# A gate handed out in two parts, six relayout transfers, single copies of R and V, and other windows for the background work

## The chip, the cores and the metric

The kernel runs on one core of a Trainium2 chip. The metric is the time of one execution on the device in microseconds (us). A core has engines that each work through their own instruction stream in order: TensorE (PE; its weight loads are listed as PEld), VectorE (DVE), ScalarE (ACT), GpSimd (POOL) and SyncE (SP), which here issues most transfers. Semaphores tie the streams together.

## The reference

Two stages in fp32. The first is a recurrence over 768 time steps for 4 batches of 8 heads, with a 40x40 state for each; the second an MLP over the 3072 tokens.

```python
for t in range(S):
    y[:, :, t] = np.einsum('bhd,bhde->bhe', rt, state)
    Sa = np.einsum('bhde,bhe->bhd', state, at)
    state_decay = state * wt[:, :, None, :] - np.einsum('bhd,bhe->bhde', Sa, bt)
    state = state_decay + np.einsum('bhd,bhe->bhde', vt, kt)
...
h = x @ w_in                       # 3072x320 by 320x2048
g = np.where(pos, h, np.where(neg, 0.0, (h + beta) ** 2 / (4.0 * beta)))
return (g @ w_out)                 # 2048 by 320
```

## The kernel before

The time steps are cut into 24 **chunks** of 32; four chunks are a **set** (0 to 5). Each chunk is worked in two halves of 16 heads.

The **chain** (`chain`) carries the state through a chunk's half in five steps of small matmuls with evictions on VectorE and ScalarE between them (L515, L525, L541, L552, L581). It needs, for the chunk, rows of a scratch in DRAM (`scr`): `load_ti` (L312, tiles `ti`) and `load_cg` (L441, L444, tiles `cg`), issued on SP; `turn` transposes them on VectorE.

The **background** prepares each set in three kinds of work, which run while earlier chunks are in the chain:
- *rows* (`prelude`): four parts a set. A part scales the inputs: a copy on ScalarE (L268), two scans on VectorE (L244), the copy of P on ScalarE (L278), three products on POOL (L279, L288, L295) and a 640 KB store to `scr` from POOL (L296). In each part `copy_rv` (L142, SP) copies a piece of R and one of V from the inputs to `scr`, 160 KB each.
- *ab* (`ab_set`): for each of four chunks a load of `tiab` by four transfers (L312), and two halves, each with two transposes on VectorE (L325), 32 small matmuls (L334) and a copy on ScalarE (L340).
- *inverse* (`invert`): after a transpose (L350) 31 steps of a product and a difference on POOL (L361, L367); `adopt` (L375) hands the result over when the set begins.

The **MoE** (`moe`) takes 64 time steps as a group (12 groups), in 8 pairs of 128-row blocks of the hidden layer. `relayout` brings a finished group's y into `X` by transfers on SP. For a pair: the first products (16 matmuls, L630, into `ph`), the gate (relu L638 and square L639 on ScalarE, minimum and maximum L640 on VectorE), its split into a high part (`gh`, L646, ScalarE) and a low part (`gl`, L647, POOL), and the second products (12 matmuls, L659). The second products of a pair are issued after the first products of the pair that follows: first products of pair k, gate of k, second products of k-1, split of k, first products of k+1.

The **order** is fixed in the program. The main loop goes through each chunk in four stages; after each it calls `fill`, which has six steps. In each step `feed(1280)` takes MoE instructions worth 1280 columns (a fill is one pair), then weights are converted by `wgen` (in the first chunks), and `background` issues rows, ab and inverse work. How much is told by `WINDOWS`: a position counts 10 for a chunk, and a kind of work of a set is spread evenly between the two positions of its window, by the weights that its generator yields (`ROWS_W`, `AB_W`, `INV_W`). The weights `AB_W[5]` and `AB_W[4]` stand after a load of `tiab` and set how much of the window passes before its first use.

Of the kernel before, what the change touches and what calls it, by code (L numbers as in the profile page):

```python
# [20 lines left out]
NB, NHD, D, L = 4, 8, 40, 32  # L21
NH = NB * NHD
# [6 lines left out]
    rows=[(0, 0), (24, 43), (38, 58), (66, 98), (106, 138)],  # L29
    ab=[(0, 0), (46, 55), (63, 79), (103, 119), (143, 159)],  # L30
    inv=[(5, 36), (55.5, 79), (81, 118), (121, 158), (161, 198)],
# [9 lines left out]
AB_W = (1, 16, 1, 4, 28, 20)  # L41
# [13 lines left out]
def rwkv_moe_kernel(ctx: ExitStack, tc: tile.TileContext, r, k, v, w, a, b, w_in, w_out, ident_d, mask_d, out):  # L55
# [83 lines left out]
    def copy_rv(s, part, c):  # L139

        x, o = ((r, O_R), (v, O_V))[part]
        nc.sync.dma_start(  # L142
            scr4[s][c, :, :, o : o + D], x.rearrange("b h (n t) e -> (b h) n t e", t=L)[:, 4 * s + c]
        )
# [103 lines left out]
    def prelude(s):  # L248
# [17 lines left out]
        for part in range(4):  # L266
# [16 lines left out]
            for i in range(2):  # L283
                copy_rv(s, i, part)
# [307 lines left out]
    def relayout(g):  # L592
# [7 lines left out]
        for i, (f, p) in enumerate(((0, 0), (1, 0), (0, 2))):  # L600
            nc.sync.dma_start(
                Xb[40 * i : 40 * i + 40, 0:4, :].rearrange("e c (b t) -> e (c b) t", b=NB),
                yf[64 * f : 64 * f + D, p : p + 2].rearrange("e p j b t -> e (p j b) t"),
            )
        for i in range(2):
            for q in range(2):
                nc.sync.dma_start(  # L607
                    Xb[40 * i : 40 * i + 40, 4 + q, :].rearrange("e (b t) -> e b t", b=NB), yf[64 : 64 + D, 2 + i, 0]
                )
        for q in range(2):  # L610
            nc.sync.dma_start(
                Xb[80:120, 4 + q, :].rearrange("e (b t) -> e b t", b=NB), yf[64 : 64 + D, 2 + q, 1]
            )
        return X
# [6 lines left out]
    def moe():  # L621
# [13 lines left out]
        def gate(k):  # L635
# [3 lines left out]
            nc.scalar.activation(gt, gt, AF.Square)  # L639
            nc.vector.scalar_tensor_tensor(out=gt, in0=gt, scalar=1.0, in1=ph, op0=ALU.min, op1=ALU.max)  # L640
            return gt
# [26 lines left out]
        for g in range(len(groups)):  # L668
            while g not in Xs:
                yield None  # L670
            for k in range(NF // 2):
# [5 lines left out]
                new = (g, k, gate(k))  # L677
                if late:
                    yield from second(*late)
                else:  # L680
                    yield 3840
# [131 lines left out]
    for c in range(1, 4):  # L813
        at(1, lambda c=c: [early_store(0, c)] + [copy_rv(0, i, c) for i in range(2)])
# [31 lines left out]
    steps += [[lambda i=i: copy_rv(1, i % 2, i // 2)] for i in range(8)] + [[lambda: pad_scr(1)]]  # L846
# [115 lines left out]
```

## Time and profile before

| | us |
|---|---|
| median of 3 runs | 881.17 |
| lowest and highest | 880.77, 887.12 |
| profiled execution, its own time | 879.51 |
| its span, first to last instruction | 877.6 |
| busy: PE, PEld | 701.3, 642.4 |
| busy: DVE, ACT, POOL | 591.9, 419.6, 441.0 |
| transfers, all queues | 122.01 MB in 222363 packets |

Busy time is the sum of an engine's instructions; since engines work side by side, the shares don't add up. A line of the page such as "L647 POOL TENSOR_TENSOR gl<-gt,gh" names the line of the kernel, the engine, the operation and the tiles. "Idle before" an instruction is time in which its engine stood still, and the name behind the arrow is what ended it. The granted clock is TensorE's, as a share of full speed (1.00 is 2.4 GHz, 0.50 is 1.2 GHz).

### The profile page before, as it was taken

The numbers are of one execution on the slowest core, as the hardware profiler recorded it, in microseconds if no ns is written. First come the engines' busy times: TensorE is split into PE (matmuls) and PEld (weight loads), VectorE is DVE, ScalarE is ACT, GpSimd is POOL, SyncE is SP. The second block draws the span as 40 slices with busy tenths as digits, with TensorE's granted clock in tenths as the row PEclk, the third lists the DMA queues.
The fourth block names the chain that finished last, engine by engine and source line by source line (L and its number), as shares of the span: only waits on it lengthen the run. The fifth ranks groups of instructions, "written<-read, shape, count | busy, mean of one in ns | idle before, by whom it ended". The sixth has DMA issues, their size and how long they took to land.

```text
span 877.6 us, 35507 instructions
## 1 busy us (share of the span) xinstructions
PE 701.3 (80%) x15360; PEld 642.4 (73%) x15360; DVE 591.9 (67%) x1338; ACT 419.6 (48%) x888; POOL 441.0 (50%) x621
## 2 busy tenths in 40 slices
PE   4225566686575996999887999888999999999994
PEld 4224555675564886888776888777899899999994
DVE  6895789778663875797475796675876777676210
ACT  6206455555531553455353455443455555555552
POOL 0300289976522587656674457763247752222331
PEclk9665656678776998999898999998999999999998
DMA  8996599888778579658577668666453554551000
GB/s 288 193 216 173 117 199 209 200 201 197 166 160 159 113 156 162 142 142 185 108 154 146 148 162 173 125 127 124 87 123 69 117 107 100 102 117 31 33 18 16
DMA packets 222363, 122.01 MB, mean 139 GB/s; under 512 B 143048, under 2 KB 214920, under 8 KB 222208
## 3 DMA queue, kind: packets, MB, share of 16 engines
q1 hardware_dynamic: 215936, 98.12, 54.4%
q0 software_dynamic: 6272, 21.63, 8.9%
q8 instruction: 121, 1.98, 1.0%
q14 instruction: 34, 0.28, 0.1%
HBM read 90.54 MB, written 27.53 MB: 135 GB/s over the span
## 4 chain that ended last, share of the span: by engine, by line
PE 48%; DVE 15%; DMA 9%; POOL 9%; SPq 7%; issue 6%; ACT 6%; DVEq 0%; ACTq 0%; POOLq 0%
PE ph L630 15%; PE po L659 14%; PE p L552 5%; DMA tiab<-scr 4%; PE p L541 3%; PE p L515 2%; POOL gl L647 2%; PE p L581 2%; SPq L312 2%; POOL lw L361 2%; PE p L525 2%; PE p L481 2%; POOL lw L367 2%; PE p L202 2%; SPq L607 2%
## 5 line engine op out<-in xcount | busy, mean ns | idle before, releaser
L647 POOL TENSOR_TENSOR gl<-gt,gh 128x512 fp32r<-128x512 f32 x96 | 125.1, 1304 | 226.3 <-ACT gh L646 226.3
L630 PE MATMUL ph<-X,w 120*128 120x256 f32 x1536 | 222.8, 298 | 4.7 <-issue 2.7
L630 PEld LDWEIGHTS ph<-X,w 120*128 120x128 f32 x1536 | 200.1, 199 | 12.8 <-issue 3.1
L659 PE MATMUL po<-w,gh 128*128 128x320 f32 x768 | 140.2, 327 | 15.9 <-ACT gh L646 15.9
L640 DVE SCALAR_TENSOR_TENSOR gt<-gt,ph 128x512 f32<-128x512 f32 x96 | 65.8, 685 | 108.9 <-ACT gt L639 91.7
L659 PEld LDWEIGHTS po<-w,gh 128*128 128x128 f32 x768 | 122.0, 200 | 19.0 <-ACT gh L646 18.3
L536 ACT ACTIVATE cg<-p 32x160 f32<-32x160 f32 x192 | 56.6, 295 | 103.3 <-PE p L525 60.2
L638 ACT ACTIVATE gt<-ph,half_c 128x512 f32<-128x512 f32 x96 | 66.0, 687 | 68.2 <-PE ph L630 67.7
L659 PE MATMUL po<-w,gl 128*128 128x320 f32 x384 | 81.4, 337 | 18.8 <-POOL gl L647 18.7
L559 DVE SCALAR_TENSOR_TENSOR cg<-p,pr 40x160 f32<-40x160 f32 x184 | 58.8, 320 | 50.8 <-PE p L552 48.8
L367 POOL TENSOR_TENSOR lw<-lw 128x31 f32<-128x31 f32 (+15 forms) x155 | 87.0, 561 | 8.5
L361 POOL TENSOR_TENSOR lw<-lw 128x31 f32<-128x31 f32 (+15 forms) x155 | 82.8, 534 | 9.3
L493 DVE TENSOR_TENSOR cg<-p,mask 32x256 f32<-32x256 f32 x192 | 80.6, 420 | 3.7 <-PE p L481 0.3
L659 PEld LDWEIGHTS po<-w,gl 128*128 128x128 f32 x384 | 65.3, 206 | 23.9 <-POOL gl L647 23.6
L552 PE MATMUL p<-cg 128*64 128x72 f32 (+1 forms) x1536 | 66.1, 246 | 0.0
L546 ACT COPY ss<-p 40x320 f32<-40x320 f32 x92 | 38.6, 420 | 55.1 <-PE p L541 53.6
L646 ACT CAST gh<-gt 128x512 fp32r<-128x512 f32 x96 | 59.6, 621 | 10.5 <-DVE gt L640 9.5
L639 ACT ACTIVATE gt<-gt 128x512 f32<-128x512 f32 x96 | 60.6, 632 | 3.1
L552 PEld LDWEIGHTS p<-cg 128*64 128x64 f32 x1536 | 60.5, 154 | 0.4 <-issue 0.4
L532 DVE SCALAR_TENSOR_TENSOR cg<-p,mask 32x128 f32<-32x128 f32 x192 | 55.2, 288 | 6.6 <-ACT cg L536 0.9
L581 PEld LDWEIGHTS p<-pr,ss 40*40 40x40 f32 x1472 | 35.7, 129 | 27.5 <-issue 20.8
L325 DVE STREAM_TRANSPOSE ea<-tiab 128x256 f32<-128x256 f32 x64 | 24.3, 418 | 46.3 <-DMA tiab<-scr 45.1
(94 smaller groups left out, 1077.7 us busy)
## 6 DMA issues: line engine op xcount, KB each, us to landing
ti<-scr SPq DMA_DIRECT2D x96, 200.0 KB
ti<-scr SPq DMA_DIRECT2D x96, 168.0 KB
scr<-arena POOLq DMA_DIRECT2D x16, 640.0 KB, 6.0
cg<-scr SPq DMA_DIRECT2D x96, 80.0 KB
X<-Y SPq DMA_DIRECT2D x36, 160.0 KB
scr<-wide SPq DMA_DIRECT2D x8, 640.0 KB
w<-in_moe_w_out_dram POOLq DMA_DIRECT2D x16, 320.0 KB, 5.4
tiab<-scr SPq DMA_DIRECT2D x32, 160.0 KB
```

The costliest lines, as they stand in the source:

```text
L361: eng.tensor_mul(t3, W3[:, 0:n, j : j + 1].broadcast_to([128, n, m]), L3[:, j + 1 :, j].unsqueeze(1).broadcast_to([128, n, m]),)
L367: eng.tensor_sub(W3[:, 0:n, j + 1 :], W3[:, 0:n, j + 1 :], t3)
L493: nc.vector.tensor_tensor(out=cg[q, f::2, C_X : C_X + 64][:, 4 * i : 4 * i + 4].rearrange("p h (j x) -> p h j x", x=32), in0=ps[quarter(f, ...
L552: nc.tensor.matmul(psv[h // 8][64 * f : 64 * f + 64, h // 2 % 4, 0:n3], lhsT=cgw[:, h * CW + C_G : h * CW + C_G + 64], rhs=cg[:, h, C_R : ...
L559: nc.vector.scalar_tensor_tensor(out=cn[er[f], f::2, C_S : C_S + D][:, halves[i]], in0=psv[i][er[f], :, 32:72], scalar=-1.0, in1=pr[er[f], ...
L630: nc.tensor.matmul(phs[k % 2][:, n * j : n * j + n], lhsT=wt[0, f // 4, wi // 2][:, wi % 2, fs], rhs=Xs[g][:, xi, :], start=i == 0, stop=i ...
L638: nc.scalar.activation(gt, ph, AF.Relu, bias=half_c, scale=0.5)
L639: nc.scalar.activation(gt, gt, AF.Square)
L640: nc.vector.scalar_tensor_tensor(out=gt, in0=gt, scalar=1.0, in1=ph, op0=ALU.min, op1=ALU.max)
L646: nc.scalar.copy(gh, gt)
L647: nc.gpsimd.tensor_sub(gl, gt, gh.bitcast(F32))
L659: nc.tensor.matmul(pos[i], lhsT=x[:, ts_], rhs=w, start=q == 0 and k == 0, stop=end)
```

## The change

Five edits. The gate is a generator in two parts: relu and square are issued after the fourth, minimum and maximum after the ninth of the second products of the pair ahead (before, all three stood ahead of the first of them). `relayout` makes six transfers of a group and not nine, with the same bytes. `copy_rv` copies R of a whole set in the first rows part and V in the second, 640 KB each; for set 0 three chunks of R, then three of V, after the three stores of rows; for set 1 one copy of each. The windows of rows, ab and inverse are others. `AB_W[4]` and `AB_W[5]` are 46 and 40 and not 28 and 20.

```diff
--- before.py
+++ after.py
@@ -26,9 +26,9 @@
 
 
 WINDOWS = dict(
-    rows=[(0, 0), (24, 43), (38, 58), (66, 98), (106, 138)],
-    ab=[(0, 0), (46, 55), (63, 79), (103, 119), (143, 159)],
-    inv=[(5, 36), (55.5, 79), (81, 118), (121, 158), (161, 198)],
+    rows=[(0, 0), (24, 43), (46, 64), (70, 90), (106, 130)],
+    ab=[(0, 0), (46, 55), (68, 84), (95, 119), (135, 159)],
+    inv=[(5, 36), (55.5, 79), (85, 118), (121, 158), (161, 198)],
 )
 
 AHEAD = 5
@@ -38,7 +38,7 @@
 SLOTS = len(SHARE)
 
 ROWS_W = (2, 2, 4, 2, 6, 6, 8)
-AB_W = (1, 16, 1, 4, 28, 20)
+AB_W = (1, 16, 1, 4, 46, 40)
 INV_W = 12
 
 TRAIL = 2.5
@@ -136,11 +136,12 @@
                 ident[rows].unsqueeze(1).broadcast_to([D, 8, D]),
             )
 
-    def copy_rv(s, part, c):
+    def copy_rv(s, part, c, n=1):
 
         x, o = ((r, O_R), (v, O_V))[part]
         nc.sync.dma_start(
-            scr4[s][c, :, :, o : o + D], x.rearrange("b h (n t) e -> (b h) n t e", t=L)[:, 4 * s + c]
+            scr[s][0 : NH * 128].rearrange("(h x) e -> h x e", x=128)[:, L * c : L * (c + n), o : o + D],
+            x.rearrange("b h t e -> (b h) t e")[:, 128 * s + L * c : 128 * s + L * (c + n), :],
         )
 
     def pad_scr(s):
@@ -280,8 +281,8 @@
             yield 1
             scan(wz, wz, dz, -1)
             rec = rows_(wz)[:, 2:10]
-            for i in range(2):
-                copy_rv(s, i, part)
+            if part < 2:
+                copy_rv(s, part, 0, 4)
             yield ROWS_W[2]
             bl = load("b", part)
             yield ROWS_W[3]
@@ -602,15 +603,12 @@
                 Xb[40 * i : 40 * i + 40, 0:4, :].rearrange("e c (b t) -> e (c b) t", b=NB),
                 yf[64 * f : 64 * f + D, p : p + 2].rearrange("e p j b t -> e (p j b) t"),
             )
+        lo = Xb[:, 4:6, :].rearrange("e q (b t) -> e q b t", b=NB)
         for i in range(2):
-            for q in range(2):
-                nc.sync.dma_start(
-                    Xb[40 * i : 40 * i + 40, 4 + q, :].rearrange("e (b t) -> e b t", b=NB), yf[64 : 64 + D, 2 + i, 0]
-                )
-        for q in range(2):
             nc.sync.dma_start(
-                Xb[80:120, 4 + q, :].rearrange("e (b t) -> e b t", b=NB), yf[64 : 64 + D, 2 + q, 1]
-            )
+                lo[40 * i : 40 * i + 40], yf[64 : 64 + D, 2 + i, 0].unsqueeze(1).broadcast_to([D, 2, NB, nt])
+            )
+        nc.sync.dma_start(lo[80:120], yf[64 : 64 + D, 2:4, 1])
         return X
 
     MM1 = ((0, 0), (1, 0), (0, 1), (2, 2), (3, 2), (2, 3), (4, 4), (5, 5))
@@ -637,8 +635,9 @@
             gt = mp.tile([128, 512], F32, tag="gt", name="gt", bufs=2)
             nc.scalar.activation(gt, ph, AF.Relu, bias=half_c, scale=0.5)
             nc.scalar.activation(gt, gt, AF.Square)
+            yield gt
             nc.vector.scalar_tensor_tensor(out=gt, in0=gt, scalar=1.0, in1=ph, op0=ALU.min, op1=ALU.max)
-            return gt
+            yield
 
         def split(gt):
             gh = mp.tile([128, 512], F32R, tag="gh", name="gh", bufs=1)
@@ -674,11 +673,13 @@
                 if late:
                     late += split(late[2])
                 yield from first(g, k)
-                new = (g, k, gate(k))
-                if late:
-                    yield from second(*late)
-                else:
-                    yield 3840
+                parts = gate(k)
+                for i, d in enumerate(second(*late) if late else (320,) * 12):
+                    yield d
+                    if i == 3:
+                        new = (g, k, next(parts))
+                    elif i == 8:
+                        next(parts)
                 late = new
         yield from second(*late, *split(late[2]))
 
@@ -811,7 +812,9 @@
     todo = {}
     at = lambda n, f: todo.setdefault(n, []).append(f)
     for c in range(1, 4):
-        at(1, lambda c=c: [early_store(0, c)] + [copy_rv(0, i, c) for i in range(2)])
+        at(1, lambda c=c: early_store(0, c))
+    for i in range(2):
+        at(1, lambda i=i: copy_rv(0, i, 1, 3))
     for k in range(AHEAD):
         at(2, lambda k=k: raw_load(k))
     at(10, lambda: [turn(0, 0, j) for j in (1, 2, 0)])
@@ -843,7 +846,7 @@
     steps += [[lambda part=part: turn_1(1, part)] for part in range(4)]
     steps += [[lambda half=half: early_ab(1, half)] for half in range(2)] + [[lambda: init_cg(2, 2)]]
     steps += [[lambda c=c: early_store(1, c)] for c in range(4)]
-    steps += [[lambda i=i: copy_rv(1, i % 2, i // 2)] for i in range(8)] + [[lambda: pad_scr(1)]]
+    steps += [[lambda i=i: copy_rv(1, i, 0, 4)] for i in range(2)] + [[lambda: pad_scr(1)]]
     first = [lambda x=x: [f() for f in x] for x in steps]
 
     def feed(cols):
```

Line numbers of the changed kernel are one higher up to the gate and a few lower or higher behind it. The first place is VectorE in the first fill of chunk 7 (L463 and L465 of the kernel before turn `ti`; L244 are scans of a rows part, L325 transposes of an ab half, L640 the gate's minimum and maximum, L583 belongs to the chain). Before:

```order
L463 STREAM_TRANSPOSE ev<-ti_83 128x512
L465 STREAM_TRANSPOSE pr_88<-ti_83 128x16x32
L325 STREAM_TRANSPOSE ea<-tiab 128x256 x2
L244 SCALAR_TENSOR_TENSOR wz<-wz,dz 128x400
L640 SCALAR_TENSOR_TENSOR gt<-gt,ph_64 128x512
L325 STREAM_TRANSPOSE ea<-tiab 128x256 x2
L583 SCALAR_TENSOR_TENSOR cg_85<-p_4692,pr_89 40x8x32 x2
```

And now:

```order
L464 STREAM_TRANSPOSE ev<-ti_83 128x512
L466 STREAM_TRANSPOSE pr_88<-ti_83 128x16x32
L326 STREAM_TRANSPOSE ea<-tiab 128x256 x4
L273 MEMSET dz 128x40
L245 SCALAR_TENSOR_TENSOR ld_w<-wz,dz 128x400
L277 COPY dz<-ld_w 128x40
L278 RECIPROCAL dz<-ld_w 128x40
L245 SCALAR_TENSOR_TENSOR wz<-wz,dz 128x400
L639 SCALAR_TENSOR_TENSOR gt<-gt,ph_64 128x512
L584 SCALAR_TENSOR_TENSOR cg_85<-p_4609,pr_89 40x8x32 x2
```

The rows part's scans and four transposes stand ahead of the gate's instruction, where two transposes and the second scan stood; the first scan of that part was in the chunk before.

The second place is ScalarE in the first two fills of chunk 9 (L519, L536 and L571 belong to the chain, L646 is the cast to the high part, L638 and L639 the gate's relu and square). Before:

```order
L519 COPY x_5735<-p_5734 128x288
L646 CAST gh<-gt 128x512
L268 COPY wz<-ld_w 128x8x40
L638 ACTIVATE gt<-ph_64,half_c 128x512
L639 ACTIVATE gt<-gt 128x512
L278 COPY arena<-ld_w 128x8x40
L571 CAST Y<-yt 128x2x4x32
L536 ACTIVATE cg_85<-p_5835 32x4x40 x2
L536 ACTIVATE cg_85<-p_5834 32x4x40 x2
```

And now:

```order
L520 COPY x_5704<-p_5703 128x288
L645 CAST gh<-gt 128x512
L636 ACTIVATE gt<-ph_64,half_c 128x512
L637 ACTIVATE gt<-gt 128x512
L572 CAST Y<-yt 128x2x4x32
L537 ACTIVATE cg_85<-p_5793 32x4x40 x2
L537 ACTIVATE cg_85<-p_5792 32x4x40 x2
```

The two copies of a rows part, L268 and L278, are gone from this chunk.

The third place is SP in chunk 7 (`scr_109` is the scratch of set 4, `scr_108` that of set 3; L664 stores the output). Before:

```order
L664 DMA out_dram<-ob 2x64x320 x2
L142 DMA scr_109<-in_r_dram 32x32x40
L142 DMA scr_109<-in_v_dram 32x32x40
L260 DMA ld_b<-in_b_dram 128x1x320
L312 DMA tiab<-scr_108 32x16x80
L312 DMA tiab<-scr_108 32x16x48
L312 DMA tiab<-scr_108 32x16x80
L312 DMA tiab<-scr_108 32x16x48
L260 DMA ld_w<-in_w_dram 128x1x320
L260 DMA ld_a<-in_a_dram 128x1x320
```

And now, with the single copy of R:

```order
L663 DMA out_dram<-ob 2x64x320 x2
L261 DMA ld_w<-in_w_dram 128x1x320
L261 DMA ld_a<-in_a_dram 128x1x320
L261 DMA ld_k<-in_k_dram 128x1x320
L148 DMA scr_109<-in_r_dram 10x4
L142 DMA scr_109<-in_r_dram 4096x1x40
L313 DMA tiab<-scr_108 32x16x80
L313 DMA tiab<-scr_108 32x16x48
L313 DMA tiab<-scr_108 32x16x80
L313 DMA tiab<-scr_108 32x16x48
L261 DMA ld_b<-in_b_dram 128x1x320
L261 DMA ld_w<-in_w_dram 128x1x320
```

The second load of `tiab` stands straight behind the copy of R, where copies of R and V and a load of b stood.

## Rows read from the trace of the kernel before

**Rows 1.** The page's busy time of each engine, with its share of the span and its instructions.

```profile
PE 701.3 (80%) x15360; PEld 642.4 (73%) x15360; DVE 591.9 (67%) x1338; ACT 419.6 (48%) x888; POOL 441.0 (50%) x621
```

**Rows 2.** Busy time of each engine by stretch, one for each chunk (from ScalarE's first copy L519 of the chunk to that of the next): chunks 7 to 15 one by one, then 18 and 19. The columns are the stretch, its length, the busy time and instructions of PE, PEld, DVE, ACT and POOL, the granted clock, the DMA share and GB/s.

```profile
334.30:373.75 39.45, 31.61 (x719) 28.47 (x718) 25.10 (x61) 15.38 (x36) 26.22 (x39) 0.87 0.74 149
373.75:399.60 25.85, 24.92 (x561) 22.98 (x562) 23.89 (x51) 15.02 (x33) 15.12 (x20) 1.00 0.64 155
399.60:434.05 34.45, 28.59 (x561) 26.27 (x562) 20.34 (x49) 14.39 (x30) 23.11 (x36) 0.85 0.66 142
434.05:464.70 30.65, 28.17 (x657) 25.66 (x658) 21.53 (x55) 16.02 (x35) 20.73 (x28) 0.94 0.73 146
464.70:503.05 38.35, 30.73 (x721) 27.79 (x722) 24.55 (x59) 15.49 (x36) 17.73 (x25) 0.91 0.75 152
503.05:528.90 25.85, 24.91 (x561) 22.97 (x562) 23.88 (x51) 15.00 (x33) 15.63 (x23) 1.00 0.68 159
528.90:561.30 32.40, 27.73 (x561) 25.48 (x561) 20.48 (x48) 14.38 (x30) 23.24 (x33) 0.89 0.68 146
561.30:589.60 28.30, 26.69 (x657) 24.20 (x658) 19.81 (x51) 14.55 (x33) 19.69 (x27) 1.00 0.74 139
589.60:625.00 35.40, 30.55 (x721) 27.73 (x722) 21.35 (x55) 14.11 (x33) 11.52 (x19) 0.90 0.49 97
...
676.10:702.10 26.00, 24.85 (x561) 22.99 (x562) 17.87 (x45) 13.76 (x31) 19.64 (x27) 1.00 0.52 110
702.10:726.50 24.40, 24.40 (x561) 22.89 (x562) 17.82 (x45) 12.97 (x29) 11.58 (x19) 1.00 0.49 97
```

**Rows 3.** Who waited for whom in the whole span: engine, line and what it waited for, then us in total, how often, the longest.

```profile
DVE gt L640 <- ACT gt L639: 91.7, 40, 4.2
ACT gt L638 <- PE ph L630: 67.7, 73, 2.7
...
DVE ea L325 <- DMA tiab<-scr: 45.1, 11, 9.0
...
PE p L334 <- DVE ea L325: 32.8, 14, 12.0
...
PE po L659 <- POOL gl L647: 18.7, 11, 6.1
...
PE po L659 <- ACT gh L646: 15.9, 12, 4.0
```

**Rows 4.** Chunk 9: five instructions of the timeline (start, length, engine, line, in brackets the idle time before it and what ended it), and two stretches as in rows 2.

```profile
399.44 2.18 PE L630 MATMUL ph<-X,w 120*128 120x256 f32 x16
...
403.10 0.69 DVE L640 SCALAR_TENSOR_TENSOR gt<-gt,ph 128x512 f32<-128x512 f32 x1 [1.64 <-ACT gt L639]
...
406.18 0.81 ACT L278 COPY arena<-ld_w 128x320 f32<-128x320 f32 x1 [3.17 <-DVE wz L244]
...
409.25 2.17 PE L659 MATMUL po<-w,gh 128*128 128x320 f32 x8 [1.70 <-ACT gh L646]
...
428.52 1.43 PE L659 MATMUL po<-w,gl 128*128 128x320 f32 x4 [4.16 <-POOL gl L647]
...
424.30:428.50 4.20, 0.06 (x1) 0.00 (x0) 0.99 (x2) 0.27 (x1) 3.96 (x7) 0.79 0.50 154
428.50:431.00 2.50, 2.48 (x38) 2.15 (x38) 0.00 (x0) 0.00 (x0) 1.90 (x3) 0.50 0.00 0
```

**Rows 5.** Chunk 7, timeline: SP's issues of copies, of b and of `tiab`, and the transpose on VectorE that waits for the last.

```profile
332.77 1.21 SPq L142 DMA_DIRECT2D scr<-in_r_dram  x1
334.02 3.68 SPq L142 DMA_DIRECT2D scr<-in_v_dram  x1
337.80 2.75 SPq L260 DMA_DIRECT2D ld_b<-in_b_dram  x1
340.65 2.13 SPq L312 DMA_DIRECT2D tiab<-scr  x4
...
347.72 0.77 DVE L325 STREAM_TRANSPOSE ea<-tiab 128x256 f32<-128x256 f32 x2 [6.95 <-DMA tiab<-scr]
```

**Rows 6.** Set 2's ab, timeline: SP's copy and load, and the first of PE's products that waited.

```profile
237.03 0.64 SPq L142 DMA_DIRECT2D scr<-in_r_dram  x1
...
238.57 1.76 SPq L312 DMA_DIRECT2D tiab<-scr  x3
...
244.95 0.68 PE L334 MATMUL p<-ea 40*32 40x32 f32 x32 [12.05 <-DVE ea L325]
```

**Rows 7.** Groups of instructions by line and form: the matmuls of all 32 halves of ab; busy us, mean ns, idle before.

```profile
L334 PE MATMUL p<-ea 40*32 40x32 f32 x1024 | 18.0, 206 | 44.4 <-DVE ea L325 32.8 <-DVE cg L583 11.6
```

**Rows 8.** A quiet fill late in the chain, timeline: the end of the gate and the cast that follows it.

```profile
810.11 0.69 DVE L640 SCALAR_TENSOR_TENSOR gt<-gt,ph 128x512 f32<-128x512 f32 x1 [0.94 <-POOL gl L647]
...
812.45 0.62 ACT L646 CAST gh<-gt 128x512 fp32r<-128x512 f32 x1
```

**Rows 9.** The issues of L607 (duration least, median, most; first and last start) and, in the tail's timeline, the two waits of PE for the last group's relayout.

```profile
L607 SPq DMA_DIRECT2D X<-Y x48: 706/707/1442, 148.3 to 831.3; - x48
...
834.10 0.38 PE L630 MATMUL ph<-X,w 120*128 120x256 f32 x1 [0.28 <-DMA X<-Y]
...
834.85 1.33 PE L630 MATMUL ph<-X,w 120*128 120x256 f32 x9 [0.36 <-DMA X<-Y]
```

**Rows 10.** The page's list of DMA issues: the store of a rows part, KB and median us from issue to landing.

```profile
scr<-arena POOLq DMA_DIRECT2D x16, 640.0 KB, 6.0
```

## The prediction

> **What bounds the kernel now.** I read the page's head first: TensorE is busy 80% of the span [rows 1], so it is a race between one long instruction stream and what holds it up. The second view is the table of stretches, cut by chunk of 32 time steps [rows 2]. In it the reader should see a floor: chunk 19, in which only the chain and the MoE run, takes 24.40 us with PE busy throughout and a granted clock of 1.00. Chunks with background work stand above it, and unevenly: chunk 8 at 25.85, chunk 9 at 34.45, chunk 11 at 38.35, chunk 15 at 35.40. The number of PE's main instructions hardly differs, so the excess is waiting and what follows from it. Third, the table of waits [rows 3]: PE stood 32.8 us before L334's products for DVE's transposes of `tiab`, and DVE itself 45.1 us for the load of `tiab`; PE stood 18.7 and 15.9 us before the second products for the low and the high part of the gate. Last, the timeline of one bad chunk [rows 4]: in chunk 9 ScalarE copies P of a rows part (L278) after a wait of 3.17 us, the gate's high part comes behind it, and PE waits 1.70 us; later GpSimd (POOL) is behind with steps of the triangular inverse and a rows part, the low part stands behind them, and PE waits 4.16 us. The granted clock, 1.00 before, is then 0.50 in the next 2.5 us of full work, which is the lower of the two levels (1.2 against 2.4 GHz): a stall costs about its length again. That is why chunk 9 has PE busy 28.59 us where chunk 8 has 24.92 [rows 2].
>
> So until chunk 16 the bound is where background steps stand in the engines' orders, and after it TensorE.
>
> **The change, part by part.** Everything is summed against the profiled execution: 879.51 us, of which 877.6 are span and 1.9 lie around it; the median of the runs is 881.17, 1.7 above.
>
> *Rows parts leave chunks 9 and 13.* With the new windows sets 4 and 5 are prepared in positions 70 to 90 and 106 to 130 instead of 66 to 98 and 106 to 138; the order of ScalarE shows chunk 9 without L268 and L278. What stays beside the inverses there is one half of an `ab` step. Nearest rows without a rows part but with ten inverse steps: chunk 18, 26.00 [rows 2]. One half of `ab` costs PE 18.0/32 = 0.56 us [rows 7]. Chunk 9: 34.45 to 26.56; chunk 13: 32.40 to 26.56. Together -13.7. Bounds: 0 (they stall for something else) and -13.7; I take the whole, because both rows name the stall and its cause leaves.
>
> *`ab` of sets 4 and 5.* Load and first use of `tiab` are put further apart in the background's count: 46 units of 362 in 24 positions, 3.0 positions, against 28 of 288 in 16, 1.6 positions. At 25 to 31 us for ten positions that is some 8 us instead of 4 to 5 (an estimate from rows 2). A load needs 340.65 to 347.72, 7.1 us, from its first issue to the transpose [rows 5]. So the wait should mostly go. Counted by the copies L340 in ScalarE's order, chunks 11 and 15 go from five halves to four. I price them by their neighbours with three halves, whose waits PE hardly saw, plus one half: chunk 11 = 30.65 + 0.56 = 31.2 (-7.1), chunk 15 = 28.30 + 0.56 = 28.9 (-6.5). Together -13.6; bounds 0 and, with both at the floor and four halves (24.40 + 4 x 0.56 = 26.64), -20.5.
>
> *Set 3.* Its halves move from chunks 6 and 7 to 7 and 8, and chunk 8 gets two rows parts. Chunk 8 then has the mix of chunk 10: 30.65 instead of 25.85, +4.8. Chunk 6 loses three halves, -1.7. Chunk 7 keeps five halves and a wait: the new order has the single copy of R straight ahead of its second `tiab` load, where a copy of R, one of V and a load of b stood; I take 0. Together +3.1; bounds -3 (chunk 7's wait goes) and +12 (chunk 8 becomes a chunk 7).
>
> *Set 2.* Its first load stood behind nine relayouts and two copies on SP, the load was issued at 238.57 and PE waited 12.05 [rows 6]. Three relayouts fewer and the copies behind the load: 3 x 0.707 [rows 9] + 1.3 (of the 1.5 from the first copy at 237.03 to the load) = -3.4. Bounds 0 and -12.1 (the whole wait).
>
> *Single copies of R and V.* Seventy instructions leave SP (the copies, 48 to 14, and the relayouts). The bytes stay. A copy of 640 KB is not in the trace of before; the nearest row is the 640 KB store of `arena`, 6.0 us to landing [rows 10]. In place of a pair of 320 KB, about 3 us, each lump keeps the `ti` and `cg` loads behind it 3 us longer in the first two parts of a set and frees them in the last two. In chunks 1 to 3, where the transfers are dense, I put +2; bounds -3 and +6. By the Trainium skill, "DMA: Bandwidth & Descriptors", section on the anatomy of one DMA, a transfer costs about 2 us fixed and its bytes at 436 GB/s, by which one copy would be an estimated 3.5 us and four 9.5; no run here shows that fit for a strided copy. By it this term would be 0 and the sum 2 us lower.
>
> *Relayout, six for nine.* In the tail PE waits 0.28 and 0.36 us for the last transfers [rows 9], which come 2.1 us sooner: -0.6. Bounds -0.6 and -2.1.
>
> *The gate in two parts.* In a fill the gate now goes out after four and nine of the second products, one to two of six background steps later. Where no background is left (chunk 17 on) nothing stands between, the order is the same and nothing can change. Elsewhere ScalarE no longer sits at the head of its queue for `ph` (67.7 us) nor VectorE for the square (91.7 us) [rows 3], but transposes and scans now stand ahead of the gate. Most of both waits is off the path. Bounds: a gain of about 15 us (what is left of PE's 34.6 us before the second products when chunks 9 and 13 are taken out, and part of the rest is conversion of weights), a loss as in the third rival. I take 0.
>
> Sum: -13.7 - 13.6 + 3.1 - 3.4 + 2 - 0.6 = -26.2. 879.5 - 26.2 = 853.3, and 1.7 for the median: **855 us**.
>
> **Rivals.**
> 1. *The stalls move.* Rows parts still meet inverses in chunks 10 and 12, and chunk 8 is crowded. If chunk 10 became a chunk 9 (+3.8), chunk 12 a chunk 13 (+6.5) and chunk 8 a chunk 11 (+7.7 more), the sum is -8: 873. For it: the same mix costs 25.85 or 34.45 by chance of order. Against it: three chunks would have to go wrong, and the spacing is wider.
> 2. *The lump of R blocks.* If each of the eight lumps of sets 2 to 5 is paid at 3 us, 24 come back: 879. The Trainium skill, the same page, section on queues, rings and completion order, says that each DMA engine consumes descriptors in ring order, which speaks against this change: a small load issued behind R waits for it. The trace agrees: in chunk 7 the `tiab` load stands 8 us behind the copies [rows 5]. Against it: that was 320 KB and a load of b; and parts 3 and 4 are free.
> 3. *Slower: the gate behind a rows part.* In nine fills of chunks 5 to 11 a whole pair of scans now stands ahead of the gate on VectorE, and the copy of P that waits for them ahead of the relu on ScalarE; before none did after chunk 4. In chunk 9 that copy ended at 406.99, 5.4 us after the first products (399.44 + 2.18), for which alone relu waits there; 1.64 of it was VectorE's wait for the square, which goes, so a relu behind the copy would be some 3.7 us late [rows 4]. The room in a quiet fill, from the end of the gate's minimum to the cast, is 812.45 - 810.80 = 1.65 us [rows 8]. If all nine pay what a late part cost chunk 9, half of its 8.45 us over chunk 18 (two stalls), 4.2 us each, 38 us are added: 893. It decides where the cast ends after the first products of the next pair.
> 4. *More than forecast.* The freed heads of both queues carry the chain too, about 15 us, and set 2's waits go, 5: 835.
>
> **How the numbers follow.** Forecast 0.54 (its own range 840 to 867), rival 1 0.15, rival 2 0.08, rival 3 0.12, rival 4 0.11. The range 835 to 881 leaves out rival 3 and the far end of rival 4. One per cent (8.8 us) is about what a measurement of this kernel can tell. Faster by more than that (below 872.4): forecast, rival 4 and a third of rival 1, 0.70. Within it: rival 2 and the rest of rival 1, 0.18. Slower (above 890.0): rival 3, 0.12.
>
> **What would show it.** By chunk, in the changed profile: 9 and 13 near 26.5; 11 and 15 near 31 and 29, with DVE's wait for `tiab` well under 45.1 us and PE's before L334 under 20; chunk 8 up to about 30; chunks 17 and on as before at 24.4 to 26. The waits of relu for `ph` and of the minimum for the square should shrink most of all, without the span following. Rival 2 shows as long SP issues behind L142 and more waiting for `ld_b`; rival 3 as PE waiting for the cast (ACT gh) in chunks 5 to 12 above 15.9 us in all. I am wrong if chunks 9 and 13 stay above 30, or if new stalls in 4 to 8 eat the gain.

## The result, and the profile of the changed kernel

| | before | after |
|---|---|---|
| median of the runs, us | 881.33 (both kernels timed on one chip) | 861.10 (860.64 to 862.11) |
| ratio of the times, with its 95% interval | | 0.9758 (0.9716 to 0.9799) |
| profiled execution, its own time | 879.51 | 861.24 |
| its span | 877.6 | 859.4 |
| mean granted clock | 0.871 | 0.883 |

The change makes the kernel 2.4% faster: 20.2 us between the medians, 18.2 between the spans. The page's first part shows that no engine has less to do; PE is busy 10.5 us less in as many instructions [rows 1], at a higher mean clock:

```profile
PE 690.8 (80%) x15360; PEld 633.3 (74%) x15360; DVE 594.3 (69%) x1338; ACT 417.5 (49%) x888; POOL 441.8 (51%) x621
```

The stretches of the changed kernel, cut and laid out as in [rows 2], from ScalarE's first copy (now L520) of a chunk to that of the next: chunks 4 to 9, then 11, 13, 15 and 19.

```profile
206.65:246.38 39.73, 29.09 (x647) 25.98 (x647) 27.28 (x60) 20.79 (x47) 15.94 (x16) 0.83 0.69 141
246.38:295.18 48.80, 32.87 (x721) 29.54 (x722) 29.24 (x64) 16.53 (x37) 18.94 (x24) 0.79 0.78 163
295.18:333.54 38.36, 29.30 (x561) 26.61 (x562) 21.81 (x51) 15.04 (x32) 30.12 (x44) 0.87 0.57 124
333.54:372.38 38.84, 32.55 (x721) 28.90 (x722) 27.06 (x64) 16.74 (x37) 29.46 (x42) 0.87 0.91 170
372.38:407.96 35.58, 29.49 (x657) 26.83 (x658) 28.54 (x58) 17.11 (x37) 15.76 (x17) 0.90 0.75 167
407.96:434.26 26.30, 25.51 (x593) 23.40 (x594) 19.18 (x49) 13.05 (x30) 18.20 (x32) 1.00 0.70 141
...
462.92:499.05 36.13, 30.90 (x677) 27.66 (x676) 25.04 (x58) 16.38 (x36) 21.01 (x32) 0.81 0.88 182
...
526.36:552.96 26.60, 25.49 (x593) 23.38 (x594) 19.16 (x49) 13.04 (x29) 18.70 (x29) 1.00 0.65 140
...
579.62:608.15 28.53, 27.11 (x689) 24.61 (x690) 20.59 (x53) 13.86 (x32) 11.56 (x19) 1.00 0.54 102
...
685.22:709.63 24.41, 24.41 (x561) 22.90 (x562) 17.84 (x45) 12.98 (x29) 11.59 (x19) 1.00 0.48 97
```

Put beside the kernel before, and beside four of the experiments that follow (us; the columns are named by their labels):

| chunk | before | after | windows_undone | copies_undone | rows3_old | store_spread |
|---|---|---|---|---|---|---|
| 4 | 50.2 | 39.7 | 49.5 | 39.8 | 49.2 | 39.2 |
| 5 | 43.5 | 48.8 | 37.9 | 47.4 | 40.2 | 46.1 |
| 6 | 30.4 | 38.4 | 29.1 | 37.4 | 30.6 | 37.6 |
| 7 | 39.5 | 38.8 | 39.8 | 38.2 | 37.0 | 37.9 |
| 8 | 25.8 | 35.6 | 25.9 | 34.3 | 36.9 | 35.2 |
| 9 | 34.5 | 26.3 | 33.8 | 26.7 | 26.8 | 25.0 |
| 10 | 30.7 | 28.7 | 26.9 | 28.7 | 28.7 | 28.7 |
| 11 | 38.3 | 36.1 | 45.7 | 32.9 | 36.0 | 33.7 |
| 12 | 25.8 | 27.3 | 25.9 | 25.8 | 27.3 | 28.9 |
| 13 | 32.5 | 26.6 | 35.6 | 26.4 | 26.5 | 25.3 |
| 14 | 28.3 | 26.7 | 27.4 | 26.1 | 27.3 | 26.1 |
| 15 | 35.4 | 28.5 | 35.3 | 28.6 | 28.0 | 28.8 |

Each column is one execution. Chunk 12, whose windows are the same in the columns after, copies_undone, rows3_old and store_spread, lies between 25.8 and 28.9 there, so a difference of 2 or 3 us in one chunk says little by itself. The column windows_undone is from the fastest of that kernel's ten executions.

The span's 18.2 us are these: chunk 0 starts 1.1 later (45.5 to 46.6), chunks 0 to 3 give 4.7 (164.7 to 160.0), chunks 4 to 15 give 13.3 (414.8 to 401.5), chunks 16 to 22 nothing, and the rest behind the start of chunk 23 gives 1.3 (76.9 to 75.6). Inside chunks 4 to 15 a gain of 37.8 us (chunks 4, 7, 9 to 11, 13 to 15) is paid back with 24.5 (chunks 5, 6, 8, 12).

The waits of the whole span, columns as in [rows 3]:

```profile
DVE gt L639 <- ACT gt L637: 87.2, 44, 3.9
...
ACT gt L636 <- PE ph L628: 58.0, 61, 2.5
...
DVE ea L326 <- DMA tiab<-scr: 31.3, 6, 13.6
PE p L335 <- DVE ea L326: 29.2, 8, 11.7
...
PE po L658 <- POOL gl L646: 20.7, 8, 6.4
...
PE po L658 <- ACT gh L645: 19.8, 16, 4.1
```

The waits for `tiab` are fewer (6 for 11) but the longest is longer (13.6 for 9.0), and PE stood before L335 almost as long as before, 29.2 us for 32.8. PE's two waits before the second products are each somewhat longer.

**Where it is lost.** Three places. In chunk 5 the second load of set 2's `tiab` is late; the timeline (start, length, engine, line, in brackets the idle time before and what ended it):

```profile
247.99 1.35 SPq L663 DMA_DIRECT2D out_dram<-ob  x2
249.43 1.22 SPq L261 DMA_DIRECT2D ld_a<-in_a_dram  x1
250.74 6.46 SPq L313 DMA_DIRECT2D tiab<-scr  x4
...
262.49 0.77 DVE L326 STREAM_TRANSPOSE ea<-tiab 128x256 f32<-128x256 f32 x2 [13.57 <-DMA tiab<-scr]
...
262.99 0.76 PE L335 MATMUL p<-ea 40*32 40x32 f32 x32 [11.70 <-DVE ea L326]
```

SP needs 6.46 us to issue four transfers that took 1.76 to 2.13 for three or four elsewhere [rows 5, 6]. In chunk 6 a rows part of set 3 now stands among the steps of set 2's inverse on POOL, and the gate's low part behind both:

```profile
305.33 1.04 POOL L296 TENSOR_TENSOR arena<-ld_b,wz 128x320 f32<-128x320 f32 x1
...
309.48 1.26 POOL L646 TENSOR_TENSOR gl<-gt,gh 128x512 fp32r<-128x512 f32 x1
...
310.80 1.43 PE L658 MATMUL po<-w,gl 128*128 128x320 f32 x4 [5.38 <-POOL gl L646]
...
328.68 0.84 PE L658 MATMUL po<-w,gl 128*128 128x320 f32 x4 [3.00 <-POOL gl L646]
```

This is the stall of the old chunk 9 [rows 4] in another chunk. And in chunk 8, which got two rows parts and three halves of ab, PE waits for `tiab`'s transposes and for the gate's high part:

```profile
380.66 0.67 PE L335 MATMUL p<-ea 40*32 40x32 f32 x32 [3.89 <-DVE ea L326]
...
403.27 1.43 PE L658 MATMUL po<-w,gh 128*128 128x320 f32 x8 [2.20 <-ACT gh L645]
```

### The profile page after: what moved, and what is told of

It is laid out like the page before. It is cut to its first block, busy times and chain, and to the rows that moved or that the text cites. A ratio compares the mean times of both kernels' runs of the same rounds, so it can differ in the third digit from the quotient of the medians.

```text
span 859.4 us, 35431 instructions
## 1 busy us (share of the span) xinstructions
PE 690.8 (80%) x15360; PEld 633.3 (74%) x15360; DVE 594.3 (69%) x1338; ACT 417.5 (49%) x888; POOL 441.8 (51%) x621
## 4 chain that ended last, share of the span: by engine, by line
PE 42%; DMA 10%; DVE 6%; POOL 5%; ACT 3%; SPq 3%; issue 2%; ACTq 0%; DVEq 0%; POOLq 0%
PE ph L628 14%; PE po L658 13%; PE p L553 4%; DMA ti<-scr 3%; PE p L542 3%; SPq L313 3%; DMA tiab<-scr 2%; PE p L516 2%; PE p L582 2%; PE p L482 2%; PE p L526 2%; DMA ld_b<-in_b_dram 2%; DMA scr<-arena 2%; POOL gl L646 1%; POOL lw L368 1%
## 5 line engine op out<-in xcount | busy, mean ns | idle before, releaser
L646 POOL TENSOR_TENSOR gl<-gt,gh 128x512 fp32r<-128x512 f32 x96 | 123.8, 1290 | 204.5 <-ACT gh L645 204.5
L628 PE MATMUL ph<-X,w 120*128 120x256 f32 x1536 | 219.1, 296 | 1.2 <-issue 1.2
L658 PE MATMUL po<-w,gh 128*128 128x320 f32 x768 | 135.9, 320 | 19.8 <-ACT gh L645 19.8
L658 PEld LDWEIGHTS po<-w,gh 128*128 128x128 f32 x768 | 117.4, 193 | 23.8 <-ACT gh L645 23.1
L639 DVE SCALAR_TENSOR_TENSOR gt<-gt,ph 128x512 f32<-128x512 f32 x96 | 65.7, 684 | 96.2 <-ACT gt L637 87.2
L658 PEld LDWEIGHTS po<-w,gl 128*128 128x128 f32 x384 | 63.7, 201 | 25.3 <-POOL gl L646 24.9
L645 ACT CAST gh<-gt 128x512 fp32r<-128x512 f32 x96 | 59.6, 621 | 10.5 <-DVE gt L639 9.5
L582 PEld LDWEIGHTS p<-pr,ss 40*40 40x40 f32 x1472 | 35.9, 129 | 30.1 <-issue 23.1
L582 PE MATMUL p<-pr,ss 40*40 40x32 f32 x1472 | 40.9, 210 | 21.1 <-DVE pr L466 16.3
```

The source lines that it names most:

```text
L582: nc.tensor.matmul(psv[er[f], p, :], lhsT=ss[er[f], p, :], rhs=pn[er[f], p, 0, 8:40], start=True, stop=True)
L628: nc.tensor.matmul(phs[k % 2][:, n * j : n * j + n], lhsT=wt[0, f // 4, wi // 2][:, wi % 2, fs], rhs=Xs[g][:, xi, :], start=i == 0, stop=i ...
L645: nc.scalar.copy(gh, gt)
L646: nc.gpsimd.tensor_sub(gl, gt, gh.bitcast(F32))
L658: nc.tensor.matmul(pos[i], lhsT=x[:, ts_], rhs=w, start=q == 0 and k == 0, stop=end)
```

## The experiments

What they had to tell apart: whether the windows alone carry the gain, or the freed queue heads of the gate (rival 4) or the fewer transfers have a part in it; whether the single copies cost what rival 2 says; and what delays the load of `tiab` in chunk 5 and lengthens chunk 11. Each is given with its median and its ratio to the kernel before on the same chip, with the 95% interval; the kernel before had 883.7, 883.1 and 883.9 in the three groups, and 881.3 beside the changed kernel. Differences in us are between medians, so across groups they are good to some 2 us; whether two kernels differ is read from the intervals.

**The tables alone**, in the kernel before:

```diff
-WINDOWS, AB_W of the kernel before
+WINDOWS, AB_W of the changed kernel
```

> The kernel before with the new WINDOWS and AB_W alone; gate, relayout and copies as before. My theory (the gain is where rows and ab stand beside the chain): 863 to 868, most of the 20 us, with chunks 9 and 13 near 26.5 and chunk 15 near 29. Rival (the shorter gate waits or the shorter SP queue carry it): 873 to 880.

864.45 us, 0.9787 (0.9747 to 0.9827), as expected, with chunks 9, 13 and 15 at 25.9, 26.7 and 28.5. The interval overlaps the changed kernel's, so the two tables by themselves give a gain of the size of the whole; the other three edits together are worth what is not told apart from nothing. It doesn't follow that each of them is worth nothing, as the next runs show.

**One edit undone at a time**, in the changed kernel: the gate, the copies, the relayout.

```diff
-parts = gate(k)
-for i, d in enumerate(second(*late) if late else (320,) * 12):
-...
+new = (g, k, gate(k))
+yield from second(*late)
```

> The changed kernel with the gate again in one piece ahead of the second products. My theory (the gate's place is worth nothing, its waits in the changed profile fell only from 67.7 to 58.0 and 91.7 to 87.2 us): 859 to 864. Rival (the gate frees the heads of ScalarE's and VectorE's queues): 868 or more. Third (the gate behind the scans costs): 856 or less.

```diff
-copy_rv(s, part, 0, 4)  # in parts 0 and 1
+for i in range(2):
+    copy_rv(s, i, part)
```

> The changed kernel with R and V copied again in pieces of 160 KB in every rows part. My theory (term of +2 for the lumps): 858 to 862. Rival (the fewer SP issues are worth something, since SP blocks behind a full queue): 865 or more. If the lump of R caused the 13.6 us wait for tiab in chunk 5, that wait falls below 9 us and the time to 855 or less.

```diff
-nc.sync.dma_start(lo[40 * i : 40 * i + 40], ...)  # 3 transfers for the low rows
+nc.sync.dma_start(Xb[40 * i : 40 * i + 40, 4 + q, :], ...)  # 6, as before
```

> The changed kernel with nine relayout transfers a group. My theory (0.6 us in the tail, a little more in set 2, where the first tiab load stands behind a relayout): 861 to 864. Rival (SP's queue is the bound before chunk 16, three issues of 0.71 us in twelve groups count): 868 or more.

Gate undone: 864.64, 0.9784 (0.9744 to 0.9825). Relayout undone: 865.46, 0.9806 (0.9772 to 0.9841). Both lie just above what I had expected (859 to 864, 861 to 864), and both intervals overlap the changed kernel's: neither edit is shown to be worth anything by itself. In the trace without the gate's edit, relu waits 65.4 us and the minimum 97.0 (58.0 and 87.2 with it). That the edit frees the queue heads is not safe to read from this pair: rows3_old, which has the edit, waits 65.5 and 98.7.

Copies undone: **854.59**, 0.9676 (0.9648 to 0.9704), below the changed kernel's interval. The single copies cost some 6.5 us. This kernel is also the tables alone plus the gate's and the relayout's edits, and on the same chip it is 9.9 us faster than the tables alone, with intervals that don't touch (0.9648 to 0.9704, 0.9747 to 0.9827). So these two edits together are worth some 10 us where the copies stay as before, and the single copies hide most of it; no run divides the 9.9 between the two. I had expected 858 to 862, and 855 or less only if the wait in chunk 5 went; it stayed at 11.80 us, so that reason fell. The stretch of chunk 11 of this kernel, columns as above, shows the largest piece:

```profile
459.59:492.44 32.85, 28.06 (x683) 25.04 (x682) 26.52 (x62) 16.30 (x37) 21.98 (x32) 0.95 0.81 188
```

32.85 for 36.13, at a clock of 0.95 for 0.81. In the changed kernel SP's issues there are these:

```profile
480.97 0.62 SPq L142 DMA_DIRECT2D scr<-in_v_dram  x1
481.91 4.79 SPq L261 DMA_DIRECT2D ld_b<-in_b_dram  x1
...
488.94 2.02 SPq L313 DMA_DIRECT2D ti<-scr  x4
```

The lump itself issues in 0.62 us; the small load behind it takes 4.79, and the chain's `ti` loads stand behind that. With the copies undone the same `ld_b` takes 1.71. But in this stretch PE has no wait above 0.73 us behind these issues. The wait that this stretch has and copies_undone has not comes before them:

```profile
478.77 0.81 ACT L279 COPY arena<-ld_w 128x320 f32<-128x320 f32 x1 [4.03 <-DMA scr<-arena]
...
482.56 1.68 PE L658 MATMUL po<-w,gh 128*128 128x320 f32 x8 [1.87 <-ACT gh L645]
...
486.00:490.00 4.00, 4.00 (x124) 3.41 (x127) 2.50 (x7) 0.85 (x3) 1.09 (x4) 0.50 0.64 123
```

ScalarE's copy of P waits until the store of the rows part before has landed, the gate's relu stands behind it, the cast is late, and PE's clock is 0.50 from 486 to 490. With the copies undone the copy of P waits 2.77 us, PE 0.33, and the clock is 1.00 there. How the lump makes the store land later (8.4 us after its issue for 6.8) no run shows, and the stretch isn't explained by this wait alone: gate_undone, with the lumps, has no such wait and 36.4 us all the same.

**Windows, weights and set 3's rows, each undone alone.**

```diff
-WINDOWS of the changed kernel, AB_W = (1, 16, 1, 4, 46, 40)
+WINDOWS of the kernel before, AB_W = (1, 16, 1, 4, 46, 40)
```

> The changed kernel with the windows of before, AB_W 46 and 40. My theory: chunks 9 and 13 stall again (34 and 32), chunk 6 back to about 30 and chunk 8 to 26; time 868 to 878. Rival (rows parts beside inverses were never the cause, the weights are): 858 to 864.

880.47, 0.9968 (0.9937 to 0.9999), above the 868 to 878 that I had expected: nearly all of the gain is gone. Its chunks 9, 13 and 15, in the trace:

```profile
390.18:423.95 33.77, 27.20 (x561) 24.84 (x562) 20.70 (x49) 14.29 (x30) 23.76 (x33) 0.90 0.53 121
...
522.44:558.03 35.59, 28.32 (x561) 25.86 (x562) 20.50 (x48) 14.26 (x30) 23.79 (x33) 0.86 0.52 115
...
585.47:620.77 35.30, 30.32 (x753) 27.51 (x754) 21.27 (x55) 14.22 (x35) 11.56 (x19) 0.90 0.51 98
```

They are back at about the old lengths and at clocks of 0.86 to 0.90 where the changed kernel has 1.00. Chunks 6 and 8 are back at 29.1 and 25.9, so the loss there belongs to the windows as well. Its chunk 11, 45.7, is longer than in either kernel: by the copies to `pairs` it holds six halves of ab there, where the kernel before has five and the changed one four, DVE waits 9.7 us for `tiab` and PE 6.2 before L335. The new weights in the old windows push a half from chunk 10 to 11, so this run is not quite the old tables' order.

```diff
-AB_W = (1, 16, 1, 4, 46, 40)
+AB_W = (1, 16, 1, 4, 28, 20)
```

> The changed kernel with AB_W 28 and 20 again, the windows new. My theory (the spacing of load and use took the waits out of sets 4 and 5): chunk 15 back above 32, chunk 11 not better, DVE's wait for tiab above 40 us in all, time 866 to 874. Rival (the windows alone, being longer for ab 4, spread them enough): 858 to 864.

867.59, 0.9807 (0.9752 to 0.9863), 6.5 us above the changed kernel but not told apart from it. The expected time came out, but not for the reason I gave: the waits for `tiab` are 28.6 us in all, under the changed kernel's 31.3, and chunk 15 stays at 28.61:

```profile
585.49:614.10 28.61, 26.93 (x689) 24.49 (x690) 19.94 (x51) 13.98 (x33) 11.54 (x19) 1.00 0.52 102
```

So chunk 15 is shorter by the new windows and needs no new weights: it holds four halves for five, and the window of ab is longer (24 positions for 16). Which of the two counts, no run tells apart. Nor is it shown that the weights are worth nothing: chunks 9 and 13 of this kernel, with the same work as in the changed one, take 28.9 and 30.1 us for 26.3 and 26.6, in one execution.

```diff
-rows=[(0, 0), (24, 43), (46, 64), (70, 90), (106, 130)],
+rows=[(0, 0), (24, 43), (38, 58), (70, 90), (106, 130)],
```

> The changed kernel with the window of set 3's rows at 38 to 58 as before, all other windows new. Theory: chunk 6 (38.4 against 30.4 before, PE waits of 5.4 and 3.0 us for the low part) is slow because a rows part of set 3 stands between the dense inverse of set 2 on GpSimd; it goes back to 29 to 32, chunks 3 to 5 pay 2 to 5 of it: 855 to 859. Rival (the inverse alone fills GpSimd there): chunk 6 stays above 36 and the time at 860 to 866.

857.23, 0.9696 (0.9648 to 0.9745): 3.9 under the changed kernel's median, with intervals that overlap. Chunk 6 is 30.6 for 38.4 and PE's wait of 5.38 us there is gone (the one of 3.00 stays), which shows that the rows part of set 3 made the long stall; chunks 3 to 5 take back 3.6 of the 7.8. The timeline of PE in chunks 4 and 5 shows how:

```profile
243.09 0.67 PE L335 MATMUL p<-ea 40*32 40x32 f32 x32 [12.35 <-DVE ea L326]
...
269.73 0.76 PE L335 MATMUL p<-ea 40*32 40x32 f32 x32 [5.00 <-DVE ea L326]
```

The wait of 12.35 us in chunk 4 is back, as it was before [rows 6], and the one of 11.70 in chunk 5 is down to 5.00. Where the rows of set 3 are prepared decides at which of set 2's two loads PE waits longer.

**The output store.** What the load of `tiab` in chunk 5 stands behind is in two traces a store of the output, two batches of 64 rows in one transfer. Split into one transfer for each batch, with the same bytes:

```diff
-nc.sync.dma_start(ov[m * i : m * i + m, t0 : t0 + nt, :], ob)
+[nc.sync.dma_start(ov[m * i + x, t0 : t0 + nt, :], ob[nt * x : nt * x + nt]) for x in range(m)]
```

> The changed kernel with each output store of 128 rows issued as two of 64 rows, same bytes. New theory: what blocks SP before the tiab load of chunk 5 (issue 6.46 us, wait 13.6) is the store ahead of it, whose 1280-byte pieces move at some 38 a us where 160-byte ones move at a thousand. Then that issue falls to about 2 us, the wait for tiab to 6 or less, the long issues of chunk 11 shrink too, and the time is 848 to 856. Rival (the queue is full of ti, cg and R): nothing or, with 24 more issues, 1 to 3 us slower: 860 to 865.

**848.48**, 0.9602 (0.9564 to 0.9641): 12.6 us less, more than any part of the change but the tables. The timeline of chunk 5 with the split store:

```profile
248.94 2.49 SPq L663 DMA_DIRECT2D out_dram<-ob  x4
...
252.20 3.00 SPq L313 DMA_DIRECT2D tiab<-scr  x4
...
259.26 0.77 DVE L326 STREAM_TRANSPOSE ea<-tiab 128x256 f32<-128x256 f32 x2 [10.14 <-DMA tiab<-scr]
```

The issue takes 3.00 us for 6.46, but the wait is still 10.14 of 13.57. I had expected it to fall to 6 or less, so the store is not the main cause of that wait. The gain lies elsewhere: 5.1 us in the tail (75.6 to 70.5 behind the start of chunk 23), some 9 spread over chunks 4 to 15. The view of transfers shows the cause best where nothing else runs, behind the last product. First the changed kernel from 853.0 to 857.5 us, then the split store from 842.9 to 844.6 (the share is of 16 DMA engines):

```profile
DMA packets 176, 0.22 MB, mean 49 GB/s; under 512 B 2, under 2 KB 176, under 8 KB 176
## 3 DMA queue, kind: packets, MB, share of 16 engines
q1 hardware_dynamic: 176, 0.22, 13.3%
```

```profile
DMA packets 201, 0.21 MB, mean 122 GB/s; under 512 B 39, under 2 KB 201, under 8 KB 201
## 3 DMA queue, kind: packets, MB, share of 16 engines
q1 hardware_dynamic: 201, 0.21, 50.4%
```

13.3% of 16 engines is the time of 2.1 engines, so the whole store seems to have gone through two, at 49 GB/s; the split one kept eight busy in the mean. SP's wait at the end for these stores was 7.4 us, with the split 1.0.

```diff
 kernel before, with the same two lines of the store and nothing else
```

> The kernel before with each output store issued as two of 64 rows. If the slow stores were what blocked SP ahead of the tiab loads already there (the copy of V at 334.02 took 3.68 us to issue, two stores stood ahead of it), the waits for tiab in chunks 5, 7 and 11 shrink and the time is 870 to 877. If they were due to the copies and loads themselves, 880 to 885.

866.38, 0.9819 (0.9769 to 0.9869), more than I had expected. In the kernel before, too, the store filled the way: the timeline around the start of chunk 7 with the split store has

```profile
328.56 4.08 SPq L664 DMA_DIRECT2D out_dram<-ob  x4
332.69 0.65 SPq L142 DMA_DIRECT2D scr<-in_r_dram  x1
333.39 0.66 SPq L142 DMA_DIRECT2D scr<-in_v_dram  x1
334.15 0.66 SPq L260 DMA_DIRECT2D ld_b<-in_b_dram  x1
334.90 2.20 SPq L312 DMA_DIRECT2D tiab<-scr  x4
```

The copy of V takes 0.66 us to issue and the load of b 0.66, where they took 3.68 and 2.75 [rows 5]. I had put these to the copies. The waits for `tiab` in chunks 5, 7 and 11 shrink as expected, from 9.0, 7.0 and 6.5 us to 4.3, 3.4 and 2.9. Chunk 7 falls from 39.5 to 35.5, chunks 11 and 15 by 3.7 and 3.9, the tail by 4.7.

**The parts that help, together.**

```diff
 changed kernel
+the split store
+copies of R and V as before (best1, best2)
+rows=[(0, 0), (24, 43), (38, 58), (70, 90), (106, 130)] (best2)
```

> The changed kernel with pieces of 160 KB for R and V again and the stores in halves. If lump and store block SP at different places, both gains add: 848.5 - 6.5 = 842. If they are the same wait seen twice: 846 to 850.

> As best1, and set 3's rows at 38 to 58. Its gain of 4 us in the changed kernel came from chunks 5 and 6 less what chunks 3 and 4 gave back. If it adds: 836 to 841. If the rows beside ab of set 2 now meet free transfers anyway: 842 or the same as best1.

846.06, 0.9571 (0.9518 to 0.9624), and **840.40**, 0.9505 (0.9456 to 0.9555). On top of the split store the copies as before bring 2.4 us more where alone they brought 6.5, which fits the second of my two expectations, one wait seen twice, but the interval of best1 overlaps that of store_spread. With the rows of set 3 as before, too, chunk 6 is at 30.6, and the kernel is 5.0% faster than before, where the change is 2.4%. This version beats the kernel before and the changed one.

```diff
 best2
-gate in two parts
+gate as before
```

> As best2, with the gate in one piece ahead of the second products. If the gate's place is worth the 3.5 us that gate_undone showed: 3 to 4 us more than best2. If it is worth nothing: within 2 us of best2.

842.25, 0.9536 (0.9497 to 0.9576). Within 2 us of best2, and the intervals overlap: here, too, the place of the gate by itself isn't shown to matter.

## Why the prediction was right, step by step

It held in time (861 for 855, inside its range) and in the view that the bound is where background steps stand in the engines' orders: windows_undone takes the gain away, tables_only gives it. The sum was -26.2 and the span moved by -18.2, and its terms did not all measure what they were put at.

That the total came so near is in part luck, since errors of both signs met in it. Read from the medians, the two tables gave 19.2 us (883.66 to 864.45) where my terms for them sum to 24.2; the gate's and the relayout's edits together gave 9.9 where I had 2.7 (0.6 in the tail and 2.1 in set 2); and the single copies cost 6.5 where I had 0.7 (2, less the 1.3 of set 2). Read by chunk, set 3 missed by 14 us and chunk 11 by 5; what lies outside the chunks that I had priced one by one (0 to 3, 10, 12, 14, the tail and the start) gave 7.0 where my terms had a loss of 1.4, and made up for part of that.

- **Rows parts leave chunks 9 and 13: right.** -14.0 (34.5 to 26.3, 32.5 to 26.6) for -13.7, at a clock of 1.00. The neighbour with the same mix, chunk 18, was the right price here, though not a safe one: with the old weights the same mix took 28.9 and 30.1. What I wrote on the way, that a stall costs about its length again, is too much: chunk 9's two stalls of 1.70 and 4.16 us [rows 4] go with 3.67 us more of PE's busy time than in chunk 8 [rows 2], 0.6 of their length. No term used it.
- **`ab` of sets 4 and 5: half right.** Chunk 15 measured 28.5 for a forecast of 28.9. Chunk 11 measured 36.1 for 31.2: the lump of R and the store stand ahead of its `tiab` load, the lump of V ahead of its `ti` loads (32.9 and 33.7 with lumps or store undone, 32.5 with both). The price by neighbours took no account of what else SP has to move there. The reason given counted the weights and the longer window as one spacing; chunk 15 keeps its gain without the weights (28.6). Chunks 10 and 14, not in the sum, gave 3.6.
- **Set 3: wrong, +17.1 for +3.1.** This is the step that failed most. I took chunk 6 to lose three halves and gain nothing, where a rows part moved in among a dense inverse, the very pattern that I had named as chunk 9's stall: +8.0 for -1.7. Chunk 8, priced by chunk 10's mix at +4.8, cost +9.8; it hasn't that mix: the old chunk 10 has one scan of a rows part and ten inverse steps, the new chunk 8 four scans and one step. Chunk 7 gave 0.7 for 0. The bound of +12 for this set did not hold.
- **Set 2: about right in sum, not in its working.** PE's first wait fell from 12.05 [rows 6] to 8.25 and chunk 4 by 10.4. Of my two parts the relayouts were right (10.12 with nine transfers, 8.25 with six, 1.9 for 2.1), the copies behind the load worth nothing (8.24 with copies as before, for 1.3). But in chunk 5 the wait grew to 11.70 from

```profile
273.06 0.77 PE L334 MATMUL p<-ea 40*32 40x32 f32 x32 [9.42 <-DVE ea L325]
```

in the kernel before, and the chunk by 5.3: -5.2 for -3.4. I had counted SP's queue alone; rows3_old shows that the rows of set 3 shift length between the two chunks. The two chunks together are 93.7 before, 88.5 after, 89.4 with the rows of set 3 as before.
- **Single copies: mis-sized and misplaced.** I put +2, in chunks 1 to 3, with a bound of +6. The undoing measured 6.5, none of it where I put it (with the copies undone chunks 0 to 3 are 1.5 longer, not shorter) and 3.3 of the span's 6.1 in chunk 11. The 0 that I quoted beside it, by a fit of fixed time and bytes, was further off.
- **Relayout: right in its two places, open in the rest.** The tail gave 1.3 for 0.6, and PE no longer waits there for the last transfers; with nine transfers the tail is 76.9 and 77.1 (tables_only, relayout_undone). Undoing it is not told apart; its part of the 9.9 us that it gave with the gate is open.
- **Gate: put at nothing, which two runs don't contradict and don't show.** Undoing it cost 3.5 and 1.9 us, not told apart either time; together with the relayout it gave 9.9. Relu and minimum did not shrink most of all, as I had written, but from 67.7 to 58.0 and from 91.7 to 87.2, where DVE's wait for `tiab` fell by 13.8.

**The rivals.** Rival 1 has the right mechanism, stalls that move, but named chunks 8, 10 and 12; they went to 5, 6 and 8, where 23.0 us were lost. Rival 2 was right that the lump blocks what stands behind it (`ld_b` 4.79 us), but at some 6.5 us in all and not 24; the 8 us that I had read for it in chunk 7 were the store's, since from the first copy to the `tiab` load it is 2.2 us in store_only. Rival 3 named PE's wait for the cast in chunks 5 to 12: it is 10.4 us there, short of 15.9, and 8.5 without the gate's edit. The stall that it described shows once, in chunk 11 (1.87 us); gate_undone, copies_undone and store_spread have no such wait above 0.8 us there. Rival 4's queue heads gave nothing that is shown for them alone. Of the signs that I named, PE's wait before L334 under 20 us failed (29.2), and so did chunk 8 at about 30 (35.6) and chunk 11 near 31 (36.1); the warning came true in part: new stalls in chunks 5 to 8 ate some of the gain.

What stays open: which of the things that rows3_old moves (loads, scans, POOL's store) makes DVE wait for the load of `tiab` in chunk 5; with the copies undone or the store split it still waits 10 us or more, and with both 8.46:

```profile
249.63 2.17 SPq L312 DMA_DIRECT2D tiab<-scr  x4
...
256.80 0.77 DVE L325 STREAM_TRANSPOSE ea<-tiab 128x256 f32<-128x256 f32 x2 [8.46 <-DMA tiab<-scr]
```

In this trace, of best1, the load takes 7.2 us from its first issue to the transpose, about as in [rows 5], and DVE stood idle before the load was issued. So what is left of this wait is no longer a long issue (2.17 us) but a load that goes out after DVE has come to it.

## What to carry to other kernels

When a table moves background work, go through every stretch that receives something and ask whether it now holds the pattern that made the old stall; here the stretches that only lost a known load came out as their neighbour had priced them, and those that received did not. Before blaming a transfer whose issue is long, look at what was issued ahead of it, and check how many DMA engines that transfer used: here the long issue was not its own. Fewer and larger background transfers were a loss here, where small urgent ones stand behind them in one queue. And undo edits in pairs too: two that are each not told apart from nothing gave 10 us together, and a third that cost 6.5 hid it.

## What was not expected of the hardware

A store of 160 KB over two batches of 64 rows (2x64x320) kept the equivalent of two of 16 DMA engines busy (13.3% share, 49 GB/s), and what stood behind it on SP took 2 to 3.5 us longer to issue (0.66 for 3.68 and 2.75, 3.00 for 6.46); split into its two batches, with the same bytes, it moved at a mean of 122 GB/s, and the changed kernel became 12.6 us, 1.5%, faster, though the four issues of two stores take 2.49 us for 1.35. The Trainium skill says in "DMA: Bandwidth & Descriptors", in the section on why a DMA increments its semaphore by 16, that a transfer runs on the largest number of engines up to 16 that divides the slowest dimension other than 1 of both its sides, by which it is two here. The trace agrees with it: 13.3% of 16 is 2.1.

A merged copy of R or V (640 KB in pieces of 160 bytes) issued in about 0.6 us in chunk 11, like a small one, and the next transfer on the same engine paid: 4.79 us for a load of b, 4.51 with the store split, and 1.71 with the copies as before. Twenty-four pairs of copies became seven, and the kernel 6.5 us slower by it.
